# K and Q transposed in one transfer, k loaded in its own order, q on GpSimd's queue, and longer latencies in the planner, in a convolution and attention kernel on one Trainium2 core

## Chip, core and metric

The kernel runs on one core of one Trainium2 chip. A core has TensorE (PE, matrix products), VectorE (DVE), ScalarE (ACT), GpSimd (POOL) and SyncE (SP, which here only issues transfers). The engines run side by side. Each takes its own instructions in the order in which they were emitted, and waits for others by semaphores. The metric is the device time of one execution in microseconds; eleven executions of the kernel before were timed, and the median counts.

## The reference, cut to what matters

Two independent halves are computed from 2048 positions of 640 channels and written side by side. The first half is a short causal filter on k with four taps, a product with v, a long convolution over the whole sequence with a direct term, and a product with q. The second is attention with 32 heads of 20 channels in four segments of 512 positions, mixed with a running memory of the segments before.

```python
for t in range(ks):
    k_shift = k_shift + k_pad[:, t:t + S, :] * shift_k[:, ks - 1 - t][None, None, :]
kv = k_shift * v
...
y_f = kv_f * kf_f[None, :, :, :]
...
return q * (y + kv * ssm_D[None, None, :])
```

```python
for s in range(N):
    logits = jnp.einsum('bhqd,bhkd->bhqk', qs, ks) * scale + mask
    p = _softmax(logits, axis=-1)
    a_dot = jnp.einsum('bhqk,bhkd->bhqd', p, vs)
    pq = phi(qs)
    num = jnp.einsum('bhld,bhde->bhle', pq, M)
    den = jnp.einsum('bhld,bhd->bhl', pq, z)[..., None] + 1e-06
    o = g * (num / den) + (1.0 - g) * a_dot
    ...
    M = M + jnp.einsum('bhld,bhle->bhde', phi(ks), vs)
return o @ wo
```

The last lines of both excerpts are drawn together here from several lines of the reference. phi(x) is x+1 for positive x and exp(x) otherwise, and the mask admits each query only to keys at or before it.

## The kernel before

**The convolution half ("A")** goes through five groups of 128 channels. In each, `load_kv` (line 574) loads v by four transfers and k, transposed, by four. The k tile `kr` holds positions apart by their remainder modulo four, so that the filter of `kshift` (line 591) reads a contiguous run of weights. The filter is 16 products of 128 columns per block of 512 positions, against `skd`, four diagonal matrices of taps. VectorE multiplies the result with v into `vt`. `fwd` turns kv, and in the same way the filter kernel (`sk`, turned to `kT`), into a spectrum with products against the table `Wf`; ScalarE copies each result from PSUM into `F`. `bfly` adds and subtracts F into `Xh` or `Kh` on VectorE. Pointwise products and a second butterfly make `S`; `inverse` multiplies with the table `Wi`, and VectorE multiplies with q (`qd`, loaded by `load_q`, line 586, four transfers on SP) into `outa`, which GpSimd's queue stores. All large tiles exist once, `outa` twice.

**The attention half ("P" and "T")** goes through eight units: four segments times two halves of 16 heads. `proj` (line 701) makes K, Q and V of 128 positions with five products of 320 columns each. ScalarE casts them into `KQ` and `Va`. Two transfers on SP turn K into `KT` and Q into `QT`, for each of four token blocks. `bound` (line 724) works out an upper bound of the logits from the maximum of K and stores it into rows of `QT`, so that the exponential cannot overflow; `PqT` is phi of Q. `attn` (line 781) runs for four groups of four heads. It writes logits of three shapes into the PSUM tile `st`, ScalarE takes the exponential into `ET`, VectorE zeroes a triangle with `cmask`, and TensorE multiplies with V into `o`. The last shape holds key block 3 (128 columns) and key block 2 (256 columns). Its mask is added by a product of 384 columns first, of which the last 128 add zeros (line 793). VectorE divides (`rr`, `o`) and writes `o_s`; `o_s` is transposed by transfers into `oT` and multiplied with `wo`; the last segment has its own ending, `out_last` (line 851).

**The order** is not that of the loops. Every call goes to a recorder (so nearly all instructions carry one source line, 441). `price` (line 182) estimates each operation's time on its engine and its latency until another engine may use the result. `plan` (line 242) then simulates the five queues forward and backward, several times. A table `BIAS` shifts priorities of single work items and a table `HOLD` moves the time before which a load may not start; both are long lists of numbers. The best of the passes sets the order in which instructions are emitted, and which of three `ab` banks in PSUM each product gets. The plan's times are not kept at run time: only the order and the semaphores are. So an estimate that is wrong does not break anything; it lets an engine wait at an instruction while a later one would be ready.

**The queues.** SP issues nearly all loads and all transposing transfers, POOL the small constants, `Drow` and the stores of `outa` and `outb`. A wait at the head of a queue holds everything behind it.

Of the kernel before, what the change touches and what calls it, by code (L numbers as in the profile page):

```python
# [25 lines left out]
KPAD = 16  # L26
# [67 lines left out]
class Recorder:  # L94
# [87 lines left out]
    def price(self, op, method, out, ins, kw):  # L182
        n = int(np.prod(list(out.shape)[1:]))
        two = lambda a: mybir.dt.size(a.dtype) == 2
        if method == "matmul":
            if "tile_position" in kw:
                op.dur += n / 2.4 * 0.33 + (200.0 if not op.dur else 0.0)
            else:
                op.dur += max(n / 2.4 + 2.5, 27.0)
            op.lat = 260.0  # L190
# [12 lines left out]
        elif op.eng == "ACT":  # L203
            op.dur, op.lat = n / 1.152 + (33 if ins[0].space == bass.MemoryType.PSUM or n > 1000 else 95), 210.0
        elif op.eng == "DVE":
            op.stall = 115 if method == "reciprocal" else 0
            fast = all(two(a) and a.space != bass.MemoryType.PSUM and int(a.ap[-1][0]) == 1 for a in [out] + ins)
            if method == "tensor_tensor":
                op.dur = n / (1.92 if fast else 0.96) + 60
            elif method == "tensor_reduce":  # L210
                op.dur = int(np.prod(list(ins[0].shape)[1:])) / 0.96 + 60
            elif method == "reciprocal":
                op.dur = 67 + 6.1 * n
            else:
                op.dur = n / (3.84 if fast else 1.9) + 60
            op.lat = 150.0
        else:
            op.dur, op.lat = 100 + n / 1.2, 200.0
# [23 lines left out]
    def plan(self, bias, hold, passes, slack):  # L242
# [19 lines left out]
        prio = [-(o.tail + bias.get(o.key, 0)) for o in ops]  # L262
        held = [hold.get(o.key, 0) if o.dma is not None else 0 for o in ops]
        for n in range(passes + 1):
            total = self.forward(prio, held)
            if best is None or total < best[0]:
                best = (total, self.order, self.slot, self.start, self.done)
# [3 lines left out]
            lead = [end - b for b in back]  # L271
            prio = [s - (bias.get(o.key, 0) >> 3) for o, s in zip(ops, lead)]
            held = [max(0, s - slack - hold.get(o.key, 0)) if l else 0 for o, s, l in zip(ops, lead, load)]
        _, self.order, self.slot, self.start, self.done = best
        return best[0]

    @staticmethod
    def lag(o):
        return o.lat if o.dma is None else max(1150 - o.dur, -50) + o.dma + 450
# [71 lines left out]
    def forward(self, prio, held):  # L351
# [19 lines left out]
        while times:  # L371
# [3 lines left out]
            for e in free:  # L375
# [27 lines left out]
                if o.dma is not None:  # L403
                    dma_free = max(dma_free, max(t + 1150, end - 50)) + o.dma
                    fin = dma_free + 450
# [44 lines left out]
class K3:  # L450
    def __init__(self, ctx, tc, A_q, A_k, A_v, A_shift_k, A_ssm_k, A_ssm_D, B_x, B_wq, B_wk, B_wv, B_wo, B_beta, out):
# [20 lines left out]
        def const(name, arr, dt, eng=nc.gpsimd):  # L472
            t = c.tile(list(arr.shape), dt, name=name)
# [8 lines left out]
        def wload(engs, half):  # L482
            def f():
                for i, (w, eng) in enumerate(zip((B_wk, B_wq, B_wv), engs)):
                    eng.dma_start(out=self.wqkv[:, :, half, i, :], in_=w.rearrange("(cc p) j -> p cc j", p=128)[:, :, 320 * half:320 * half + 320])
# [6 lines left out]
        }  # L492
        self.skc = c.tile([128, 5, 4], bf16, name="skc")
        nc.sync.dma_start(out=self.skc[:], in_=self.shift_k.rearrange("(c p) t -> p c t", p=128))
        self.ident = const("ident", np.eye(128).astype(BF16_NP), bf16, nc.sync)
        bt = self.bt = c.tile([128, H], bf16, name="bt")
# [4 lines left out]
        self.nmask = const("nmask", np.concatenate([(cmask_np.astype(np.float32) - 1) * 30000.0] * 2 + [np.zeros((128, 128), np.float32)], axis=1).astype(BF16_NP), bf16)  # L501
        self.epsrow = const("epsrow", eps_np, f32)

        self.KQ = c.tile([128, 2, 2, 16, 32], bf16, name="KQ")
        self.PK = c.tile([128, 4, 16, 32], bf16, name="PK")
        self.Va = [c.tile([128, 4, 16, VW], bf16, name=f"Va{i}") for i in range(2)]
        self.QT = [c.tile([128, 4, L], bf16, name=f"QT{i}") for i in range(2)]
# [43 lines left out]
    def a_chunks(self, dp):  # L551
# [22 lines left out]
        def load_kv():  # L574
# [3 lines left out]
            kr = st["kr"] = self.ring("kr", [128, 4, KPAD + 512])  # L578
            nc.gpsimd.memset(kr[:, :, 0:KPAD], 0.0)
            for c in range(4):  # L580
                nc.sync.dma_start_transpose(out=kr[:, c, KPAD:KPAD + 512], in_=self.k[:, dsl].rearrange("(r c) d -> r c d", c=4)[:, c, :])
# [4 lines left out]
        def load_q():  # L586
            qd = st["qd"] = self.ring("qd", [128, 4, 4, 128])
            for b in range(4):
                nc.sync.dma_start(out=qd[:, b], in_=self.q[512 * b:512 * b + 512, dsl].rearrange("(p c) d -> p c d", c=4))

        def kshift(b):
            def f():
                kr, vt = st["kr"], st["vt"]
                ps = self.bank("ab")
                for c in range(4):
                    for t in range(4):
                        cc = (c - t) % 4
                        p0 = KPAD + 128 * b + (c - t - cc) // 4
                        nc.tensor.matmul(ps[:, 128 * c:128 * c + 128], lhsT=kr[:, cc, p0:p0 + 128], rhs=st["skd"][:, t, :], start=(t == 0), stop=(t == 3))
# [90 lines left out]
    def b_proj_chunks(self, u):  # L690
# [10 lines left out]
        def proj(tci):  # L701
            def f():
# [9 lines left out]
                if tci == 0:  # L712
                    self.KTs[u] = self.ring("KT", [128, 4, L], n=2)
                nc.sync.dma_start_transpose(out=self.KTs[u][:, :, tok], in_=KQ[:, 0, :, :])
                nc.sync.dma_start_transpose(out=QT[:, :, tok], in_=KQ[:, 1, :, :])
# [8 lines left out]
        def bound():  # L724
            kam = self.ring("kam", [128, 4], f32)
            V.tensor_reduce(out=kam[:], in_=self.KTs[u][:], axis=AX.X, op=ALU.max, apply_absolute_value=True)
            A = self.ring("A", [128, 4, 16])
            V.tensor_tensor(out=A[:], in0=self.sel[:], in1=kam[:, :, None].to_broadcast([128, 4, 16]), op=ALU.mult)
            if s > 0:
                nc.scalar.activation(out=PqT[:], in_=QT[:], func=ACTF.Exp)  # L730
                tq = self.ring("tq", [128, 4, L])
                V.tensor_scalar(out=tq[:], in0=QT[:], scalar1=1.0, scalar2=1.0, op0=ALU.add, op1=ALU.max)
                V.tensor_tensor(out=PqT[:], in0=PqT[:], in1=tq[:], op=ALU.min)
            qabs = self.ring("tq", [128, 4, L])
            V.tensor_scalar(out=qabs[:].bitcast(i16), in0=QT[:].bitcast(i16), scalar1=0x7fff, scalar2=None, op0=ALU.bitwise_and)
# [38 lines left out]
    def b_attn_chunks(self, u):  # L774
# [6 lines left out]
        def attn(g):  # L781
            def f():
# [5 lines left out]
                for spec, e0, step in ((((0, 0),), 0, -1), (((1, 0),), 512, 1), (((3, 0), (2, 128)), 896, -1)):  # L788
                    st = self.bank("st")
                    masked = e0 == 896  # L790
                    if masked:
                        for hl in range(4):
                            nc.tensor.matmul(st[:, hl, 0:384], lhsT=self.ident[:], rhs=self.nmask[:], start=True, stop=False)
                    for (kc, c0) in spec:
                        for hl in range(4):
                            rows = slice(32 * hl, 32 * hl + 32)
                            nc.tensor.matmul(st[:, hl, c0:c0 + L - 128 * kc], lhsT=KT[rows, g, 128 * kc:128 * kc + 128], rhs=QT[rows, g, 128 * kc:L],
                                             start=not masked, stop=(not masked or kc == 2), tile_position=(32 * hl, 0))
# [82 lines left out]
    ('A', 0, 0): 157004, ('A', 0, 1): 10101, ('A', 0, 10): -7597, ('A', 0, 11): 3913, ('A', 0, 12): 33761, ('A', 0, 13): -3728, ('A', 0, 14): 5624,  # L881
    ('A', 0, 15): 88348, ('A', 0, 16): 230629, ('A', 0, 17): -8128, ('A', 0, 18): -5757, ('A', 0, 19): 10830, ('A', 0, 2): 8829, ('A', 0, 20): 4481,
    ('A', 0, 21): 1304, ('A', 0, 22): -3994, ('A', 0, 23): 145, ('A', 0, 24): -576, ('A', 0, 25): -2524, ('A', 0, 26): -1099, ('A', 0, 27): -2858,
    ('A', 0, 3): 16866, ('A', 0, 4): -698, ('A', 0, 5): -458, ('A', 0, 6): 389434, ('A', 0, 7): 607, ('A', 0, 8): 3517, ('A', 0, 9): -8145,
    ('A', 1, 0): -1731, ('A', 1, 1): 3601, ('A', 1, 10): -137531, ('A', 1, 11): -176854, ('A', 1, 12): -7874, ('A', 1, 13): -16279, ('A', 1, 14): 10588,
    ('A', 1, 15): 2905, ('A', 1, 16): -7, ('A', 1, 17): -2655, ('A', 1, 18): -2590, ('A', 1, 19): -1545, ('A', 1, 2): 1649, ('A', 1, 20): 40028,
    ('A', 1, 21): 1391, ('A', 1, 22): 3816, ('A', 1, 23): -2584, ('A', 1, 24): -7, ('A', 1, 25): -2923, ('A', 1, 26): 731, ('A', 1, 27): 396,
    ('A', 1, 3): 395, ('A', 1, 4): -322, ('A', 1, 5): 12977, ('A', 1, 6): 7861, ('A', 1, 7): -1057, ('A', 1, 8): -201, ('A', 1, 9): 261,
    ('A', 2, 0): -69696, ('A', 2, 1): -2356, ('A', 2, 10): -15708, ('A', 2, 11): 257, ('A', 2, 12): -55, ('A', 2, 13): 1762, ('A', 2, 14): 6674,
    ('A', 2, 15): 491, ('A', 2, 16): 243, ('A', 2, 17): -2104, ('A', 2, 18): 175, ('A', 2, 19): 3992, ('A', 2, 2): -3416, ('A', 2, 20): 250546,  # L890
    ('A', 2, 21): -2544, ('A', 2, 22): -615, ('A', 2, 23): -563, ('A', 2, 24): -3861, ('A', 2, 25): 952, ('A', 2, 26): 5253, ('A', 2, 27): -3491,
    ('A', 2, 3): -2503, ('A', 2, 4): -4457, ('A', 2, 5): 2480, ('A', 2, 6): 5034, ('A', 2, 7): -2075, ('A', 2, 8): 243, ('A', 2, 9): -346,
    ('A', 3, 0): -36045, ('A', 3, 1): 546, ('A', 3, 10): 150040, ('A', 3, 11): -1390, ('A', 3, 12): 2538, ('A', 3, 13): -590, ('A', 3, 14): 898,
    ('A', 3, 15): 3192, ('A', 3, 16): -3627, ('A', 3, 17): -3799, ('A', 3, 18): -1242, ('A', 3, 19): 12597, ('A', 3, 2): 492, ('A', 3, 20): -88007,
    ('A', 3, 21): 959, ('A', 3, 22): -5393, ('A', 3, 23): -3393, ('A', 3, 24): -1459, ('A', 3, 25): 91621, ('A', 3, 26): 73805, ('A', 3, 27): 18751,
    ('A', 3, 3): -1299, ('A', 3, 4): -1550, ('A', 3, 5): -2302, ('A', 3, 6): 1825, ('A', 3, 7): 239, ('A', 3, 8): -4198, ('A', 3, 9): 1989,
    ('A', 4, 0): 7225, ('A', 4, 1): 3377, ('A', 4, 10): -14537, ('A', 4, 11): 1258, ('A', 4, 12): -875, ('A', 4, 13): -2828, ('A', 4, 14): -1432,
    ('A', 4, 15): 3521, ('A', 4, 16): 902, ('A', 4, 17): 30, ('A', 4, 18): -2548, ('A', 4, 19): 10489, ('A', 4, 2): -568, ('A', 4, 20): 140696,
# [107 lines left out]
```

The softmax here doesn't subtract the row's maximum and nothing guards it: scores larger than these inputs give would overflow.

## Time and profile before

| what | value |
|---|---|
| median of 11 executions | 334.29 us (329.99 to 337.91) |
| the profiled execution | 329.31 us |
| its span | 327.5 us |
| granted TensorE clock, mean | 0.986 |
| DMA traffic | 35.67 MB, mean 109 GB/s |
| packets under 512 B | 90000 of 97160 |
| KT<-KQ and QT<-KQ on SP | 32 each, 1.22 us an issue, 2.5 us to landing |
| kr<-in_A_k_dram on SP | 20, 1.26 us an issue, 2.8 us to landing |
| qd<-in_A_q_dram on SP | 20, 0.62 us an issue, 3.3 us to landing |

The span is the profiled execution from its first to its last instruction. Busy time of an engine is the time in which at least one instruction of it runs. A row of the groups gives an operation, its output and inputs, its count, its busy time, and the mean of one in ns; the means overlap their neighbours, so they sum to more than the busy time. A matmul's record includes its latency, so its rate is read from a run of them: sixteen of 128 columns take 0.90 us.

### The profile page before, as it was taken

Reading aid. Unit: us, or ns where it says so; the run is one execution under the profiler, and the core shown is the slowest. Engines: PE = TensorE matmul, PEld = TensorE weight load, DVE = VectorE, ACT = ScalarE, POOL = GpSimd, SP = SyncE. Lnnn points to the kernel's source line nnn. Section 1 sums busy time; section 2 is a strip of 40 time slices with the busy share of each in tenths; the row PEclk is TensorE's granted clock in tenths of the full one; section 3 lists DMA queues with packets and bytes.
Section 4 is the critical chain, followed back from the end, with each engine's and each line's share of the span. In section 5 each row is a group of like instructions: output and inputs, shape, how many; then the busy total and the mean of one; then the engine's idle time right before and its main releaser. Section 6 shows DMA issues by size and latency. Waiting matters only on the chain. (4 is left out here: it accounts for less than half of the span.)

```text
span 327.5 us, 8830 instructions
## 1 busy us (share of the span) xinstructions
PE 284.7 (87%) x3674; PEld 197.5 (60%) x3674; DVE 272.5 (83%) x455; ACT 265.7 (81%) x351; POOL 30.5 (9%) x58
## 2 busy tenths in 40 slices
PE   0498899989999996999999997999989988887982
PEld 0365667676777674566858664777756664654641
DVE  0016869999998979999997599999999999989842
ACT  1176799799998999899898898888899999668611
POOL 5001100000000110000101010300200002321310
PEclk9999999999999999899999999999999999998898
DMA  8945964646407987805321669513314244233262
GB/s 253 228 89 122 261 118 83 129 118 114 80 2 163 196 135 157 234 16 81 68 64 45 122 137 184 153 29 70 66 35 67 60 59 97 58 84 106 64 128 82
DMA packets 97160, 35.67 MB, mean 109 GB/s; under 512 B 90000, under 2 KB 95168, under 8 KB 96864
## 3 DMA queue, kind: packets, MB, share of 16 engines
q1 hardware_dynamic: 94816, 30.01, 44.2%
q0 software_dynamic: 1872, 4.76, 5.5%
q8 instruction: 29, 0.48, 0.6%
q10 hardware_dynamic: 432, 0.34, 0.3%
q14 instruction: 11, 0.09, 0.1%
HBM read 13.46 MB, written 5.24 MB: 57 GB/s over the span
## 5 line engine op out<-in xcount | busy, mean ns | idle before, releaser
L441 ACT ACTIVATE ET<-st 128x1536 bf16<-128x1536 f32 (+1 forms) x96 | 154.8, 1613 | 23.4 <-PE st L441 22.9
L441 PE MATMUL ab<-wqkv,xT 128*128 128x320 bf16 x480 | 76.4, 306 | 13.2 <-DMA wqkv<-in_B_wk_dram 12.4
L441 PEld LDWEIGHTS <-xT 128*128 128x128 bf16 x480 | 45.3, 100 | 33.3 <-DMA xT<-in_B_x_dram 10.4
L441 PEld LDWEIGHTS <-ET 128*128 128x128 bf16 x1280 | 42.2, 96 | 11.4 <-issue 8.1
L441 PE MATMUL o<-Va,ET 128*128 128x21 bf16 x1280 | 44.1, 173 | 3.6 <-DVE o L441 3.3
L441 ACT CAST F<-ab 128x512 bf16<-128x512 f32 x80 | 45.3, 613 | 1.8 <-PE ab L441 1.6
L441 PE MATMUL st<-QT,KT 32*128 32x128 bf16 (+3 forms) x512 | 34.9, 304 | 8.5 <-ACT ET L441 8.3
L441 ACT CAST KQ<-ab 128x320 bf16<-128x320 f32 x64 | 27.9, 459 | 15.1 <-PE ab L441 14.6
L441 DVE TENSOR_TENSOR S<-S 128x2048 bf16<-128x2048 bf16 (+1 forms) x40 | 36.9, 938 | 0.0
L441 PEld LDWEIGHTS <-Wf 128*128 128x128 bf16 x320 | 28.1, 97 | 11.2 <-issue 7.3
L441 PE MATMUL st<-nmask,ident 128*128 128x384 bf16 x128 | 26.6, 331 | 2.6 <-ACT ET L441 2.5
L441 PEld LDWEIGHTS <-KT 32*128 32x128 bf16 x512 | 11.8, 92 | 28.2 <-issue 26.3
L441 PE MATMUL ab<-kT,Wf 128*128 128x256 bf16 x160 | 23.6, 273 | 0.9 <-ACT F L441 0.2
L441 POOL DMA_DIRECT2D out_dram<-outa x20 | 15.3, 769 | 93.8 <-DVE outa L441 86.0
L441 PE MATMUL ab<-wo,oT 128*128 128x320 bf16 (+1 forms) x140 | 21.5, 292 | 2.7 <-ACT outb L441 1.7
L441 DVE TENSOR_TENSOR o<-o,rr 128x320 bf16<-128x320 f32 x48 | 23.1, 482 | 0.5
L441 DVE TENSOR_TENSOR ET<-ET,cmask 128x1024 bf16<-128x1024 bf16 x32 | 21.5, 673 | 1.8 <-ACT ET L441 1.8
L441 DVE TENSOR_TENSOR S<-Xh,Kh 128x4096 bf16<-128x4096 bf16 x10 | 22.8, 2275 | 0.0
L441 PE MATMUL ab<-vt,Wf 128*128 128x256 bf16 x160 | 22.0, 273 | 0.8 <-DVE vt L441 0.5
L441 PE MATMUL ab<-S,Wi 128*128 128x256 bf16 x160 | 20.7, 273 | 0.8 <-DVE outa L441 0.8
L441 PEld LDWEIGHTS <-oT 128*128 128x128 bf16 x160 | 13.9, 98 | 12.1 <-issue 4.9
L441 PE MATMUL ab<-skd,kr 128*128 128x128 bf16 x320 | 20.7, 219 | 0.5 <-DVE vt L441 0.4
(70 smaller groups left out, 393.5 us busy)
## 6 DMA issues: line engine op xcount, KB each, us to landing
sk<-in_A_ssm_k_dram SPq DMA_DIRECT2D x5, 512.0 KB, 4.2
vt<-in_A_v_dram SPq DMA_DIRECT2D x20, 128.0 KB, 3.1
qd<-in_A_q_dram SPq DMA_DIRECT2D x20, 128.0 KB, 3.3
out_dram<-outa POOLq DMA_DIRECT2D x20, 128.0 KB, 2.6
out_dram<-outb POOLq DMA_DIRECT2D x12, 160.0 KB, 2.9
Wf<-c_wf SPq DMA_DIRECT2D x1, 1024.0 KB
Wi<-c_wi SPq DMA_DIRECT2D x1, 1024.0 KB
wqkv<-in_B_wq_dram SPq DMA_DIRECT2D x2, 400.0 KB, 5.7
```

The costliest lines, as they stand in the source:

```text
L441: f(*[fix(a) for a in args], **{k: fix(v) for k, v in kw.items()})
```

## The change

Five edits are made at once.

1. K and Q of a token block are turned into one tile `KQT` by one transfer, where there were two. The first unit is turned by TensorE, with `ident`, into PSUM, and copied out by VectorE (K) and ScalarE (Q).
2. k is transposed by two transfers of 1024 positions in their own order. The filter reads weights with a step of four.
3. q is loaded by GpSimd's queue.
4. The mask product of the third shape has 256 columns. Key block 2's product is split into two of 128 columns, of which the second needs no mask and starts its own accumulation.
5. The planner assumes longer latencies (products 300 ns, ScalarE 320, VectorE 240 with 8 ns more for each operation, transfers 800 ns after the last packet), dearer first and cheaper later row-tiled products, applies `BIAS` and `HOLD` in one last pass after the others, and gives constants, the three weights of each half, `kr` and `skd` keys of their own. Both tables are replaced throughout.

```diff
-                op.dur += n / 2.4 * 0.33 + (200.0 if not op.dur else 0.0)
+                op.dur += n / 2.4 * 0.26 + (200.0 if not any("tile_position" in c[3] for c in op.calls[:-1]) else 0.0)
...
-            op.lat = 260.0
+            op.lat = 300.0
...
-            op.dur, op.lat = n / 1.152 + (33 if ins[0].space == bass.MemoryType.PSUM or n > 1000 else 95), 210.0
+            op.dur, op.lat = n / 1.152 + (33 if ins[0].space == bass.MemoryType.PSUM or n > 1000 else 95), 320.0
...
-            op.lat = 150.0
+            op.dur += 8
+            op.lat = 240.0
...
-        prio = [-(o.tail + bias.get(o.key, 0)) for o in ops]
-        held = [hold.get(o.key, 0) if o.dma is not None else 0 for o in ops]
+        prio = [-o.tail for o in ops]
+        held = [0] * len(ops)
...
+        return self.forward([p - bias.get(o.key, 0) for p, o in zip(prio, ops)],
+                            [max(0, t - hold.get(o.key, 0)) if l else 0 for t, o, l in zip(held, ops, load)])
...
-                    fin = dma_free + 450
+                    fin = dma_free + 800
...
-            kr = st["kr"] = self.ring("kr", [128, 4, KPAD + 512])
-            nc.gpsimd.memset(kr[:, :, 0:KPAD], 0.0)
-            for c in range(4):
-                nc.sync.dma_start_transpose(out=kr[:, c, KPAD:KPAD + 512], in_=self.k[:, dsl].rearrange("(r c) d -> r c d", c=4)[:, c, :])
+            kr = st["kr"] = self.ring("kr", [128, KPAD + S])
+            nc.gpsimd.memset(kr[:, 0:KPAD], 0.0)
+            for n in range(2):
+                nc.sync.dma_start_transpose(out=kr[:, KPAD + 1024 * n:KPAD + 1024 * n + 1024], in_=self.k[1024 * n:1024 * n + 1024, dsl])
...
-                nc.sync.dma_start(out=qd[:, b], in_=self.q[512 * b:512 * b + 512, dsl].rearrange("(p c) d -> p c d", c=4))
+                nc.gpsimd.dma_start(out=qd[:, b], in_=self.q[512 * b:512 * b + 512, dsl].rearrange("(p c) d -> p c d", c=4))
...
-                        nc.tensor.matmul(ps[:, 128 * c:128 * c + 128], lhsT=kr[:, cc, p0:p0 + 128], rhs=st["skd"][:, t, :], start=(t == 0), stop=(t == 3))
+                        first = KPAD + 512 * b + c - t
+                        nc.tensor.matmul(ps[:, 128 * c:128 * c + 128], lhsT=kr[:, first:first + 509:4], rhs=st["skd"][:, t, :], start=(t == 0), stop=(t == 3))
...
-                nc.sync.dma_start_transpose(out=self.KTs[u][:, :, tok], in_=KQ[:, 0, :, :])
-                nc.sync.dma_start_transpose(out=QT[:, :, tok], in_=KQ[:, 1, :, :])
+                self.KTs[u] = self.KQT[half][:, 0]
+                if u > 0:
+                    nc.sync.dma_start_transpose(out=self.KQT[half][:, :, :, tok].rearrange("p i g t -> p (i g) t"), in_=KQ.rearrange("p i h d -> p (i h d)"))
+                else:
+                    for i in range(2):
+                        ps = self.bank("ab")
+                        for g in range(4):
+                            nc.tensor.matmul(ps[:, 128 * g:128 * g + 128], lhsT=KQ[:, i, 4 * g:4 * g + 4, :], rhs=self.ident[:], start=True, stop=True)
+                        (V.tensor_copy if i == 0 else nc.scalar.copy)(out=self.KQT[half][:, i, :, tok], in_=ps[:].rearrange("p (g t) -> p g t", g=4))
...
-                            nc.tensor.matmul(st[:, hl, 0:384], lhsT=self.ident[:], rhs=self.nmask[:], start=True, stop=False)
-                    for (kc, c0) in spec:
+                            nc.tensor.matmul(st[:, hl, 0:256], lhsT=self.ident[:], rhs=self.nmask[:], start=True, stop=False)
+                    parts = [(kc, c0, 0, L - 128 * kc) for kc, c0 in spec] if not masked else [(3, 0, 0, 128), (2, 128, 0, 128), (2, 128, 128, 256)]
```

What this makes of the order, as it stands in the lists of instructions of the two kernels: SP begins with Wf, sk, xT, wq, wk, ident, wv before, and with wk, wq, xT, wv, ident, skc, sk after, Wf following as the ninth. ScalarE's last copy of F for the first butterfly of kv has 45 of its instructions ahead before, and 76 after. VectorE's first butterfly of the filter kernel has 8 ahead before, and 41 after. In the end of the list, two of the last four `outa` products stand behind the last `o_s` after the change, where all four stood ahead.

## The prediction

> **What bounds the kernel now.** I read the page's busy times first, then busy time by stretch, then the waits, then the chain that ended last, and the start and the end of the timeline.
>
> ```profile
> PE 284.7 (87%) x3674; PEld 197.5 (60%) x3674; DVE 272.5 (83%) x455; ACT 265.7 (81%) x351; POOL 30.5 (9%) x58
> ...
> 12.44:46.50 34.06, 30.37 (x307) 21.69 (x306) 17.26 (x34) 24.84 (x45) 2.28 (x5) 1.00 0.66 147
> 46.50:315.70 269.20, 249.56 (x3338) 173.47 (x3335) 253.28 (x417) 238.01 (x302) 23.67 (x38) 0.99 0.47 97
> 315.70:327.50 11.80, 4.73 (x35) 2.24 (x33) 1.96 (x4) 1.60 (x4) 0.21 (x1) 0.90 0.38 96
> ```
>
> Three engines are above 80%, so the whole span says little. The stretches do: each line has the stretch, its length, then PE, PEld, DVE, ACT and POOL busy. Before 46.5 us VectorE worked 17.26 us; from there, the first butterfly of kv, to the last write of o_s at 315.7 it worked 253.28 of 269.20 us, 94.1%, against PE's 92.7% and ACT's 88.4%. So in the long stretch VectorE is nearest to its limit, PE just behind.
>
> ```profile
> PE ab L441 <- DMA wqkv<-in_B_wk_dram: 12.4, 1, 12.4
> DVE rr L441 <- PE o L441: 6.6, 10, 2.2
> DVE outa L441 <- PE ab L441: 3.3, 5, 1.2
> ACT PqT L441 <- DMA QT<-KQ: 2.8, 3, 1.1
> DVE kam L441 <- DMA KT<-KQ: 0.8, 1, 0.8
> ```
>
> The waits, from the whole trace (total, times, longest): one start of 12.4 us for weights, and about 10 us in which VectorE waits for PE's attention and inverse products. Waits for the transposed K and Q are small: 2.8 and 0.8 us.
>
> ```profile
> PE 19%; DVE 11%; ACT 4%; DMA 3%; issue 2%; DVEq 0%; SPq 0%; ACTq 0%
> ...
> 1.63 5.67 SPq L441 DMA_TRANSPOSE xT<-in_B_x_dram  x1
> 7.36 0.57 SPq L441 DMA_DIRECT2D wqkv<-in_B_wq_dram  x1
> 7.98 0.52 SPq L441 DMA_DIRECT2D wqkv<-in_B_wk_dram  x1
> ...
> 46.51 1.23 DVE L441 TENSOR_TENSOR Xh<-F 128x2048 bf16<-128x2048 bf16 x1 [0.64 <-ACT F L441]
> ```
>
> The chain, which reaches back only to 200 us, has 3% of the span in DMA and none in SP's queue: unloading SP is worth little by itself. The timeline shows the start: xT's issue holds SP for 5.67 us and the first weights come behind it. Its last line is the butterfly, released by ScalarE's last copy of F.
>
> **The Trainium skill.** Three places bear on this.
> - "TensorE: Matmul & The Clock Gate", Part 3 (The mechanism): products on different row groups of the array run together. The trace agrees: four 32-row products of 512 columns take 0.28 to 0.33 us from their start to the next work.
> - "SBUF — State Buffer", the trap on DVE and DMAs of the GpSimd queue: GpSimd writes those descriptors and is locked out while VectorE runs in a 2-port mode. The trace shows a little at most: out_dram<-outa takes POOL 750 ns at least and 944 at most.
> - "DMA: Bandwidth & Descriptors", Issuing engines are not separate DMA queues: another queue saves only sequencer time, because all share the same DMA engines. For qd that time is 20 issues, 14.0 us summed on SP's timeline. The sharing itself no view of mine isolates.
>
> **The change part by part.**
>
> *Mask columns.* Four mask products of 384 columns take 0.81 us with a record of 0.33, so they follow at (0.81-0.33)/3 = 0.16 us; 256 columns at the same rate take 0.107. 128 of them save 128 x 0.053 = 6.8 us of PE. Against it, key block 2's product is split: 12 instructions replace 8, with the same columns. The 8 took 0.28 us from start to next work, so three fours take 0.28 to 0.42; over 32 groups that is 0 to 4.5 us, and I take 1.5. PE: -5.3 us.
>
> *First unit on TensorE.* 32 products of 128 columns at 0.056 (16 of kr's take 0.90): +1.8 us PE. Four VectorE copies of PSUM at 0.69 (row of ET<-st, 128x512), after overlap with neighbours 2.5 us; four ScalarE copies at 0.61, 2.2 us. All lie before 30 us, where VectorE is mostly idle. They save the first unit's eight transfers of 1.2 us on SP.
>
> *One transfer for K and Q.* 56 issues of 1.22 us become 28 of twice the size. This size is not in the trace; it lies between 1.22 (no dearer) and 2.44 (no saving). xT is five times KT's size and takes 2.75 to 3.25, so interpolation gives about 1.6. Q lands later by 0.4, never earlier than K's old transfer plus its own. Since the waits for both sum to 3.6 us, I book 0, bounds -2 to +2.
>
> *k in its own order.* Twenty issues of 1.25 become ten of about 1.6. TensorE now reads weights at a step of four elements. sk is read so already: 113 ns a load against 98 for kr, but four take 0.26 us and sixteen of kr 0.90, both near 0.05 apart. Cost 0, bound 320 x 0.015 = 4.8 us.
>
> SP's timeline, summed, is 209 us; these parts and qd take about 67 off. It is hidden already, so 0.
>
> *qd on POOL.* Twenty issues of 0.76 add 15 us to POOL's 30.5. In the new order each group of four after the first stands between outa stores of the channel group before. They wait for that group's last multiplication, since qd has one buffer, and up to 3 us of stores queue behind. outa has two buffers, and the next inverse comes tens of us later. Cost 0; if a late qd held the inverse, VectorE would wait behind it, up to 2 us for each of five groups.
>
> *Start.* SP's new order is wk, wq, xT, wv, and only then sk and Wf (1.5 MB, ahead of xT before). xT issues at about 1.9 us instead of 1.63 but with less in front. It landed 8.7 us after its issue; without Wf and sk I take 6.3, bounds 4.5 and 8.7. The first product comes at 8.2 us instead of 12.44, and the first cast at 9.7.
>
> *Order.* This decides. I count work ahead of marks in each engine's instruction list, mean durations scaled so that totals meet busy times (ACT 0.885, DVE 0.902). Before's first butterfly of kv has 16.7 us of VectorE work ahead by this count; 17.26 were measured. In the changed list it has 28.3, because k's butterfly, two bounds and more attention stand ahead. Its last F copy stands behind 46.6 us of ScalarE work counted from the first cast (before: 24.8).
>
> ScalarE's 16.4 us ahead of the first exponential are paced by PE: 75 projection products at 0.139, 32 turns, 16 of sk, 20 of kT, bound and memory, 17.1 us, at 85% 20, so the first exponential is at 28.5. The remaining 30.2 at 97% (it ran at 99% from 34.7 to 46.5) end at 59.6; I take 59.0. VectorE has then idled 59.0-28.3 = 30.7 us, against 46.5-17.3 = 29.2: a 1.5 us loss.
>
> From there to o_s VectorE has 272.5+2.5-28.3-3.2 = 243.5 us; the 3.2 are the last copies and two outa products that now stand after o_s, under the transfer of oT. At 94.1% that takes 258.8 us. But more attention and projection is done by then: PE has 281.2 less 46 (8.2 to 59 at 91%) less 5 for the tail = 230 us left, 0.945 of VectorE's work instead of 0.985, and ScalarE 218, 0.90 instead of 0.94. If PE can be filled to 92.7% as before, VectorE reaches 243.5/(230/0.927) = 98.1%. Dependences will not let all of it come; I take halfway, 96.1%, or 253.4 us.
>
> *Sum.* 59.0+253.4 = 312.4, plus the unchanged tail of 11.8 = 324.2 us of span, 326.0 with the 1.8 around it, against 329.3: -3.3. The profiled execution was below all eleven timed runs. I carry the difference to their median: 334.3-3.3 = **331.0 us**.
>
> **Rivals.**
> - *Late butterfly, slower.* If ScalarE holds F back behind the exponentials of the first unit, the first butterfly comes at 62.5, and if VectorE's share stays 94.1% the sum is 62.5+258.8+11.8+1.8 = 334.9, +5.6, median 339.9. For it: the changed list has about 30 ScalarE instructions more ahead of that F. Against it: PE and ScalarE have less left. It decides from 57 us on at the old share, or below 94.9% at 59.
> - *No change.* Longer assumed latencies only shuffle the list, VectorE's share becomes 94.9%, and 59.0+256.6 puts o_s back at 315.6: 334.3.
> - *Full release.* xT early, first butterfly at 56.5, VectorE at 98.1%: 56.5+248.2+13.6 = 318.3, -11.0, median 323.3. Stretches at 97 to 99% between 60 and 100 and 200 and 260 us of the old trace speak for it; single buffers for S, F, vt and qd against.
>
> **How the numbers follow.** Forecast 0.46 (its own range 328 to 333.5), full release 0.12, no change 0.13, late butterfly 0.29. Under 0.5%, 1.7 us, this kernel's measurement tells nothing from no change. The forecast's range crosses that a little, so faster 0.55, same 0.15, slower 0.30. The range 321.5 to 339.5 reaches from full release to the late butterfly and takes in qd's and the weight loads' bounds.
>
> **What would show it.** PE busy near 281, DVE 275; first product near 8 us; first Xh<-F near 59; VectorE's share from there to the last o_s near 96%; waits for KQT under 5 us; POOL issues of qd under 1 us. A share under 95%, a first butterfly after 61, or inverses that wait for qd make the forecast wrong.

## The result and the profile after

The changed kernel took 335.34 us (median of 12 executions, 333.58 to 338.15), beside 333.05 us for the kernel before (47 executions). The ratio is 1.0094, 95% interval 1.0064 to 1.0124: slower by about 1%, where 331.0 us and a gain were forecast. Ratios, here and below, are taken over the executions within 1.5% of each kernel's fastest, which leaves out more of the kernel before than of the others, so they can lie up to 0.9% above the ratio of the medians. The profiled execution took 335.37 us, its span is 333.6 us.

The page of the changed kernel, busy times and the granted TensorE clock in 40 slices:

```profile
PE 284.8 (85%) x3834; PEld 202.0 (61%) x3834; DVE 275.9 (83%) x459; ACT 268.3 (80%) x355; POOL 46.3 (14%) x78
...
PEclk9999999999799999999699999999999999997598
```

VectorE and ScalarE do what was forecast (275 and about 268), and POOL's 16 us more are qd. TensorE was to fall to 281 and stayed at 284.8. The clock row has a dip in its eleventh slice, one in its twentieth and a longer one near the end.

Busy time by stretch, cut at the marks of the prediction: first product, first exponential, first butterfly of kv, end of the last o_s. The columns are those explained in the prediction, and the one after POOL is the granted clock.

```profile
0.00:11.07 11.07, 0.00 (x0) 0.00 (x1) 0.00 (x0) 1.28 (x1) 5.38 (x17) 1.00 0.81 187
11.07:33.18 22.11, 21.61 (x168) 14.56 (x169) 10.30 (x23) 15.55 (x35) 0.00 (x0) 1.00 0.47 154
33.18:64.02 30.84, 29.52 (x419) 21.29 (x418) 18.82 (x36) 29.99 (x42) 1.09 (x3) 1.00 0.77 138
...
64.02:321.20 257.18, 228.13 (x3204) 162.66 (x3203) 243.44 (x394) 219.87 (x275) 38.36 (x56) 0.95 0.47 92
321.20:333.60 12.40, 5.50 (x47) 3.47 (x45) 3.38 (x7) 1.61 (x4) 1.50 (x2) 0.89 0.34 95
```

The first butterfly comes at 64.0 us, not 59.0. From there VectorE has 243.44 us of work, as counted (243.5), and does it in 257.2 us, a share of 94.7% where 96.1% was taken; the kernel before had 94.1%. The tail is 12.4 us instead of 11.8. So the 9.4 us between the forecast span (324.2) and the measured one are 5.0 of a late butterfly, 3.8 of share, and 0.6 of tail. A first butterfly after 61 us and a share under 95% were both on the prediction's list of signs that it is wrong.

Between the medians the miss is only 4.3 us (335.34 for 331.0). The profiled execution of the kernel before lay 5.0 us under the median of its eleven, and that of the changed kernel lies at its own, so the two profiles differ by more than the two kernels do.

TensorE had 228.13 us of work in the long stretch, where 230 were counted, and was busy for 88.7% of it; the kernel before had 92.7%. So VectorE was not held up by more work on TensorE than was forecast. Both engines waited more.

The waits over the whole trace (total, times, longest), those that answer to the prediction's:

```profile
PE ab L442 <- DMA xT<-in_B_x_dram: 11.1, 1, 11.1
...
DVE rr L442 <- PE o L442: 6.8, 10, 2.1
...
DVE outa L442 <- DMA out_dram<-outa: 2.3, 1, 2.3
...
ACT KQ L442 <- DMA KQT<-KQ: 1.8, 1, 1.8
...
DVE tq L442 <- DMA KQT<-KQ: 0.9, 1, 0.9
...
ACT PqT L442 <- DMA KQT<-KQ: 0.5, 1, 0.5
```

The start now waits for xT instead of weights. The waits for KQT sum to 3.2 us, about what those for K's and Q's separate transfers did before (3.6). One new wait, 2.3 us of VectorE for the store of outa, lies in the tail. The chain of work that ended last tells more of KQT than the waits do:

```profile
DVE 35%; PE 31%; ACT 15%; DMA 11%; issue 6%; SPq 1%; POOL 0%; DVEq 0%; ACTq 0%; POOLq 0%
PE ab L442 22%; DVE S L442 9%; ACT ET L442 7%; DMA KQT<-KQ 6%; PE st L442 5%; DVE Xh L442 5%; PE o L442 4%; DMA xT<-in_B_x_dram 3%; ACT F L442 3%; DVE Kh L442 3%; DVE ET L442 2%; DVE o L442 2%; DVE F L442 2%; DVE outa L442 2%; DVE kam L442 2%
```

For 6% of the span, some 20 us, it runs through the transfer KQT<-KQ. Small waits do not put a transfer off the path. (This chain reaches back to the start; that of the kernel before reached only to 200 us, so the shares of the two cannot be compared.)

### The profile page after: what moved, and what is told of

Its sections match the earlier page's. It is cut to its first block, busy times and chain, and to the rows that moved or that the text cites. A ratio compares the mean times of both kernels' runs of the same rounds, so it can differ in the third digit from the quotient of the medians.

```text
span 333.6 us, 9034 instructions
## 1 busy us (share of the span) xinstructions
PE 284.8 (85%) x3834; PEld 202.0 (61%) x3834; DVE 275.9 (83%) x459; ACT 268.3 (80%) x355; POOL 46.3 (14%) x78
## 4 chain that ended last, share of the span: by engine, by line
DVE 35%; PE 31%; ACT 15%; DMA 11%; issue 6%; SPq 1%; POOL 0%; DVEq 0%; ACTq 0%; POOLq 0%
PE ab L442 22%; DVE S L442 9%; ACT ET L442 7%; DMA KQT<-KQ 6%; PE st L442 5%; DVE Xh L442 5%; PE o L442 4%; DMA xT<-in_B_x_dram 3%; ACT F L442 3%; DVE Kh L442 3%; DVE ET L442 2%; DVE o L442 2%; DVE F L442 2%; DVE outa L442 2%; DVE kam L442 2%
## 5 line engine op out<-in xcount | busy, mean ns | idle before, releaser
L442 ACT CAST F<-ab 128x512 bf16<-128x512 f32 x80 | 44.0, 604 | 3.0 <-PE ab L442 2.9
L442 ACT CAST KQ<-ab 128x320 bf16<-128x320 f32 x64 | 26.7, 437 | 20.5 <-PE ab L442 18.2
L442 PE MATMUL st<-KQT 32*128 32x128 bf16 (+2 forms) x640 | 36.1, 283 | 6.7 <-ACT ET L442 6.5
L442 PEld LDWEIGHTS <-KQT 32*128 32x128 bf16 x640 | 13.2, 93 | 24.2 <-issue 22.1
L442 PE MATMUL st<-nmask,ident 128*128 128x256 bf16 x128 | 20.0, 280 | 8.6 <-ACT ET L442 8.6
L442 PE MATMUL ab<-vt,Wf 128*128 128x256 bf16 x160 | 22.7, 278 | 1.1 <-DVE xm L442 0.9
L442 PE MATMUL ab<-S,Wi 128*128 128x256 bf16 x160 | 21.5, 280 | 0.0
L442 DVE RECIPROCAL rr<-o 128x16 f32<-128x16 f32 (+1 forms) x64 | 15.2, 238 | 6.8 <-PE o L442 6.8
L442 PEld LDWEIGHTS <-kr 128*128 128x128 bf16 x320 | 19.1, 114 | 2.4 <-issue 2.1
```

Source lines behind the costliest of these rows:

```text
L442: f(*[fix(a) for a in args], **{k: fix(v) for k, v in kw.items()})
```

## The experiments

All ratios are to the kernel before, executed on the same chip in turn with each experiment. Experiments 1 to 4 ran on one chip, 5 to 8, 9 and 10, 11 and 12, and 13 to 16 on others. Ratios from different chips are less certain than their intervals say: e11 and e16 are the same kernel, with medians of 331.70 and 332.23 us, and their ratios are 0.993 (0.990 to 0.997) and 1.000 (0.998 to 1.003). Where an order is kept while the code is edited, the planner's call is replaced by a list:

```diff
-    rec.plan(BIAS, HOLD, PASSES, SLACK)
+    rec.fixed(ORDER)
```

**Order and edits apart.** e1 has all edits (with the first unit turned by transfer too) in the old order. e2 and e3 are the same code, with one kernel's order up to the first Xh and the other's for the rest.

> All five code edits (one KQ transfer, k in its own order, q on GpSimd's queue, the narrower mask, and the first unit also by transfer instead of TensorE), but every operation stands where the kernel before has it in its order. Theory 1 (the order of the ramp costs, the edits are neutral or a small gain): 0.98 to 1.00 of the time before, first Xh near 46.5 us, VectorE's share after it near 94%. Theory 2 (the edits cost: longer landing of KQT, q on GpSimd, weights at a step): 1.005 to 1.015, with waits for KQT above 6 us. Theory 3 (a lower granted clock, brought by the edits): the clock is 0.96 here too and PE's busy time does not fall below 284 us.

> The same code as e1. The order is that of the kernel before up to the four butterflies that write the first Xh, and that of the changed kernel for all that is left. Theory 1 (the ramp of the new order costs): first Xh near 46.5 us, at or below e1's time, 0.98 to 0.995 of before. Rival (the long stretch of the new order costs): 1.00 to 1.02, more than e1, VectorE's share after the first Xh under 94%. Theory 2: as in e1, about 1.01.

> The same code as e1. The order is that of the changed kernel up to the four butterflies that write the first Xh, and that of the kernel before for what is left. Theory 1: first Xh near 64 us, 1.005 to 1.02 of before, more than e1 and e2. Rival (the long stretch of the new order costs): 0.98 to 1.00. Theory 2: about 1.01, like e1.

Measured: e1 1.037 (1.031 to 1.043), e2 1.038 (1.033 to 1.043), e3 1.074 (1.069 to 1.080). The edits in the old order cost four times what the whole change costs. Theory 2 had the waits for KQT, but not this size. The waits of VectorE in e1:

```profile
DVE kam L456 <- DMA KQT<-KQ: 9.5, 4, 4.3
DVE kam L456 <- issue: 7.9, 3, 4.1
```

kam, the maximum of K, stands in the old order where K's own transfer landed early. Now K comes with Q, and VectorE waits 17.4 us in all at this instruction (before: 1.4), with all its later work behind. For 9.5 us of that the profile names KQT's transfer, for 7.9 it shows no releaser. The signs of theory 3 are there as well: the clock is 0.958 over all executions, and TensorE's busy time 284.2 us. But e5 below, without the single transfer, has 0.987 and 279.6 us, so the low clock came with the waits and not with the other edits.

e2 and e3 carry the same wait (5.6 and 19.1 us) and a seam between two orders, so they don't decide between ramp and long stretch. One thing e2 does show: its first Xh came at 46.9 us, but the first S<-Xh,Kh, the product made of it, only at 82.1 (70.7 in the changed kernel), and it took 346.8 us. An early first butterfly gains nothing where the work behind it does not move up.

**The start.** e4 is the changed kernel with this edit and SP's order as the expectation says:

```diff
-            nc.sync.dma_start_transpose(out=xT[:], in_=self.x[L * s:L * s + L, :])
+            for t in range(4) if s == 0 else ():
+                nc.sync.dma_start_transpose(out=xT[:, :, 128 * t:128 * t + 128], in_=self.x[128 * t:128 * t + 128, :])
```

> The changed kernel with the first segment's xT brought by four transfers of 128 positions instead of one of 512, in SP's order xT0, wk, xT1, wq, wv, xT2, xT3. All else as changed. If the 5 us that the first butterfly came too late stem from the landing of xT, the first product comes at 6.5 to 8 us instead of 11.1, the first Xh 3 to 4 us earlier than 64.0, and the time is 0.997 to 1.002 of before (after: 1.009). If the ramp is held by ScalarE and dependences instead, the first product comes earlier but the first Xh by under 1 us, and the time stays within 1.005 to 1.012.

Measured: 0.997 (0.994 to 1.000), 332.72 us. SP's first issues (start, length), of the changed kernel and then of e4:

```profile
0.74 0.46 SPq L442 DMA_DIRECT2D wqkv<-in_B_wk_dram  x1
1.25 0.51 SPq L442 DMA_DIRECT2D wqkv<-in_B_wq_dram  x1
1.82 5.70 SPq L442 DMA_TRANSPOSE xT<-in_B_x_dram  x1
```

```profile
0.74 1.32 SPq L456 DMA_TRANSPOSE xT<-in_B_x_dram  x1
2.11 0.57 SPq L456 DMA_DIRECT2D wqkv<-in_B_wk_dram  x1
2.74 1.21 SPq L456 DMA_TRANSPOSE xT<-in_B_x_dram  x1
```

The one large transfer is issued at 1.82 us and released the first product at 11.07, 9.2 us later. With a quarter of it, TensorE starts at 6.97 us, released by wk. The first Xh comes at 61.3 us instead of 64.0; of 4.1 us at the start 2.7 arrive there, a little less than the 3 to 4 expected, in part because TensorE then waits 0.8 us for wq. The gain is 1.2% by the ratios and 0.8% by the medians (332.72 for 335.34 us, other chips), and fits the first reading. e4 changes two things at once, though: its transfers are smaller, and the first of them stands ahead of all weights. One whole xT in first place was not run, so which of the two counts is not shown.

**Which edit needs which order.** e5 is e1 without the single KQ transfer. e6 is the changed kernel with two transfers again. e7 has q on SP, e8 is the kernel before with the mask edit alone.

```diff
-                    nc.sync.dma_start_transpose(out=self.KQT[half][:, :, :, tok].rearrange("p i g t -> p (i g) t"), in_=KQ.rearrange("p i h d -> p (i h d)"))
+                    for i in range(2):
+                        nc.sync.dma_start_transpose(out=self.KQT[half][:, i, :, tok], in_=KQ[:, i, :, :])
```

> The kernel before, in its own order, with the narrower mask, k in its own order and q on GpSimd's queue, but with K and Q in two transfers as before. In e1 the maximum of K (kam) waited 17.4 us for KQT where it waited 1.4 us before. If the single transfer is what made e1 slow, the time is 0.985 to 1.00 and kam waits under 2 us. If q on GpSimd or k's weights at a step did it, 1.02 to 1.04 as e1.

> The changed kernel in its order, with K and Q of all units but the first in two transfers into KQT, K's right behind its cast and Q's where the single one stands. If the single transfer still costs in the new order, 0.995 to 1.005 of before (after: 1.009). If the new order has already hidden its landing (waits for KQT sum to about 3.5 us in the trace of after), 1.005 to 1.013.

> The changed kernel in its order with q loaded on SP, at the same places of the list. If qd on GpSimd's queue costs (late stores of outa and late qd), 0.998 to 1.006. If it was free, as predicted, 1.007 to 1.014.

> The kernel before in its own order with the narrower mask alone. The prediction's 5.3 us less of TensorE work, in an order that waits for VectorE in the long stretch: 0.99 to 1.00 of before, PE busy 279 to 281 us. If the work that is saved comes back through a lower granted clock, PE busy stays near 284 us and the time at 0.997 to 1.003.

Measured: e5 0.993 (0.990 to 0.997), kam waits 1.2 us. e6 1.033 (1.026 to 1.039), outside both expectations. e7 1.012 (1.006 to 1.018). e8 0.998 (0.995 to 1.002), TensorE busy 278.9 us.

In the old order the single transfer is more than the whole loss: e1 against e5 is 4.4% by the ratios, and e5, with the other three edits, is faster than the kernel before. What of it is the later landing, what the wait for Q's cast, and what the tile that K and Q now share, no run separates. In the new order the single transfer is worth about 2%: e6 took 341.78 us, and e7, which equals the changed kernel in time, 335.34 on the same chip. SP's timeline shows where most of this arises. In the ramp of e6 the eight half-size issues where four stood keep SP busy nearly without a gap, and what stands behind them slips. The same issue, the bound's rows for the second unit, in the changed kernel and in e6:

```profile
52.60 0.62 SPq L442 DMA_DIRECT2D KQT<-bT  x1
```

```profile
36.48 4.41 SPq L456 DMA_TRANSPOSE KQT<-KQ  x3
...
47.57 4.72 SPq L456 DMA_TRANSPOSE xT<-in_B_x_dram  x1
52.38 3.01 SPq L456 DMA_TRANSPOSE kr<-in_A_k_dram  x2
...
56.93 0.62 SPq L456 DMA_DIRECT2D KQT<-bT  x1
```

It comes 4.3 us later, TensorE's weight loads wait 2.6 us for kr, and the first Xh is at 68.2 us, 4.2 later than in the changed kernel. I placed K's transfer right behind its cast; another place might cost less, so the 2% is what the single transfer is worth against this placement.

q on GpSimd is free within the interval. The mask edit takes 5.8 us off TensorE and nothing off the kernel that the ratio shows; the medians (331.57 for 333.90 us) leave room for 0.7%. k in its own order and q on GpSimd's queue together did gain in the old order: on the same chip, with 22 executions each, e5 took 329.49 us and e8, which lacks them, 331.57. Resampling the executions puts this at 0.2 to 1.0%.

**The start in the old order.** e9 is e5 with xT in four and the weights ahead of Wf and sk, edited as e4.

> e5 (old order, narrower mask, k in its own order, q on GpSimd's queue, K and Q in two transfers) with the first segment's xT in four transfers and SP starting with xT0, wk, xT1, wq, wv, xT2, xT3, ident, sk, Wf. If the start is on the path as e4 showed in the new order, the first product comes near 7 us instead of 12.4 and the time is 0.975 to 0.985 of before (e5: 0.993). If the old order's ramp is held by sk and Wf, which now come later, the first Xh stays near 46.5 us and the time at 0.99 to 1.00.

Measured: 0.993 (0.990 to 0.996), as e5. The first product comes at 6.4 us, but TensorE then waits 2.5 us for wq and 3.0 for sk, and the first Xh is at 48.6 us instead of e5's 47.4. The second reading holds: the old order feeds its ramp with what was pushed back.

**The granted clock.** Over all executions its mean was 0.959 for the changed kernel, 0.979 to 0.980 for the kernel before, 0.987 for e5. Two stretches of the changed kernel, and what lies around them:

```profile
80.00:84.00 4.00, 0.96 (x19) 0.32 (x16) 3.97 (x4) 3.45 (x3) 2.67 (x4) 1.00 0.78 188
84.00:89.00 5.00, 4.63 (x46) 2.90 (x47) 4.21 (x11) 2.37 (x4) 0.00 (x0) 0.66 0.04 13
89.00:160.00 71.00, 62.77 (x915) 45.27 (x912) 68.78 (x111) 66.43 (x84) 7.16 (x11) 1.00 0.56 109
160.00:168.00 8.00, 7.36 (x74) 3.84 (x74) 7.78 (x15) 6.05 (x8) 0.77 (x1) 0.57 0.01 2
```

TensorE is busy for 0.96 of the 4 us from 80 to 84, because it waits for an exponential of ScalarE and then for the bound (A); near 156 us it waits for an exponential once, for longer:

```profile
82.11 0.40 PE L442 MATMUL st<-KQT 32*128 32x512 bf16 x4 [1.55 <-ACT ET L442]
84.36 1.10 PE L442 MATMUL ab<-tq,A 128*16 128x512 bf16 x4 [1.85 <-DVE A L442]
...
158.28 0.60 PE L442 MATMUL st<-nmask,ident 128*128 128x256 bf16 x4 [2.79 <-ACT ET L442]
```

Then the clock is at half for some 3.4 us (a mean of 0.66 over 5), and VectorE, fully busy until then, idles for 0.8 of 5 us. The Trainium skill, "TensorE: Matmul & The Clock Gate", Part 1 (The HAM clock gate), says that an idle window of about 3.4 us halves the clock, and a busy one restores it. The trace agrees in length, and shows that TensorE need not be idle for that long: two gaps of 1.55 and 1.85 us with 0.4 us of work between them sufficed, and one of 2.79. In the kernel before the clock falls at 130 us, after one gap of 2.27.

What decides is a fixed grid of windows. In every profiled execution, each stretch at half or at full clock, from the first entry of the clock in the trace to the last fall, lasts a whole multiple of 3.413 us. Cut into such windows from that entry on, all eighteen executions together show this: after a window at full clock in which TensorE was busy for less than 46% the clock was halved (36 of 36), after one of more than 72% never (0 of 1392), and between the two it went both ways (19 of 109). At half clock, a window under 89% busy left it halved (53 of 53). Where the grid lies differs between executions, so the same gap may or may not matter: the changed kernel has no fall after a gap of 1.74 us at 274 us, and e13, with the same instructions, has one after 1.75 us at 278.

The longest fall lies near the end of the changed kernel, and no run removed it:

```profile
300.00:317.00 17.00, 9.68 (x137) 5.91 (x136) 16.89 (x26) 11.27 (x9) 2.40 (x4) 0.61 0.19 53
```

From 303.6 to 317.3 us the clock is at half, and as long or longer in e4 and in each of e10 to e16; the kernel before has 3.4 us there. VectorE is busy for 16.89 of the 17 us, so what this fall costs can't be read from the stretch, and it was not tested.

e10 is e4 with products that nothing reads added near 80 and 156 us; e12 is e10 with wq earlier. e11 and e14 to e16 put them into the changed kernel itself, and e13 is their base, without them.

```diff
+    rec.add_banks("warm", [rec.slots["o"][0]])
+    for i, n in enumerate(WARM):
+        rec.key = ("warm", i)
+        ps = rec.bank("warm")
+        for _ in range(n):
+            rec.nc.tensor.matmul(ps[:, 384:512], lhsT=K.ident[:], rhs=K.ident[:], start=True, stop=True)
```

WARM is (34, 18, 42): 34 and 18 products ahead of the first two instructions shown above, 42 ahead of the third (e14 has only the first two numbers, e15 only the last). They write columns of the bank `o` that are otherwise unused.

> e4 (changed kernel with xT in four) with 94 products of ident with ident added, whose result nothing reads, at the places where TensorE waited 1.3 to 2.8 us just before its granted clock fell to 0.5: 52 of them near 78 to 82 us, 42 near 153 us. If the halved clock costs time, it stays at 1.00 from 80 to 90 and from 155 to 165 us and the time is 0.990 to 0.996 of before (e4: 0.997). If VectorE is the bound where the clock falls, the clock stays up as well but the time stays at 0.995 to 1.001.

> The changed kernel itself (xT in one transfer) with the same 94 unread products at the same two places of its list as in e10, and nothing else. If the fall of the granted clock at 84 and 160 us is part of what VectorE's share lost, the mean clock rises from 0.96 to about 0.97 and the time is 1.002 to 1.006 of before (after: 1.009). If the clock falls only where VectorE is the bound, 1.007 to 1.012.

> e10 with wq issued ahead of the second quarter of xT (SP: xT0, wk, wq, xT1, wv, xT2, xT3). In e4 TensorE waited 0.81 us for wq after its first five products. If that wait is on the path, the first Xh comes 0.5 to 0.8 us earlier than 60.6 and the time is 0.989 to 0.994 of before. If the second quarter of xT is late instead, 0.994 to 1.000.

> The changed kernel with its own order written out instead of planned: the same instructions. It is the base for e14 to e16 on the same chip: 1.005 to 1.013 of before, clock 0.953 to 0.963.

> e13 with the 52 unread products near 80 us only. The fall of the clock at 84 us left VectorE idle for 0.8 us of the four after it. If that fall costs time, 1 to 2.5 us less than e13. If VectorE's later idle time swallows it, less than 0.7 us.

> e13 with the 42 unread products near 156 us only. VectorE was 0.97 to 1.00 busy while the clock was down there, so 0 to 0.7 us less than e13 if VectorE is what bounds that stretch; 1.5 us or more if TensorE's backlog is met later, in the stretch of 220 to 240 us, where VectorE idles 4.6 us.

> e13 with all 94 products, as e11. By the medians of e10 and e11 3.5 us less than e13, that is 0.998 to 1.001 of before. If the ratios' smaller figure holds, 0.5 to 1 us less.

| run | us | ratio | 95% interval | mean clock |
|---|---|---|---|---|
| e10 | 329.35 | 0.995 | 0.992 to 0.998 | 0.975 |
| e11 | 331.70 | 0.993 | 0.990 to 0.997 | 0.972 |
| e12 | 329.33 | 0.984 | 0.978 to 0.989 | 0.974 |
| e13 | 336.00 | 1.013 | 1.008 to 1.017 | 0.957 |
| e14 | 332.90 | 1.002 | 1.000 to 1.005 | 0.965 |
| e15 | 334.03 | 1.007 | 1.005 to 1.010 | 0.966 |
| e16 | 332.23 | 1.000 | 0.998 to 1.003 | 0.970 |

By the ratios e10 gained 0.2% over e4 and e11 1.6% over the changed kernel, on different chips (by the medians 3.4 and 3.6 us); e13 to e16 settle it on one. Against e13, products at the first place save 3.1 us, at the second 2.0, at both 3.8, though the 94 add 5.3 us of TensorE work (94 at 0.056). e11, e12 and e14 gained more than was expected of them. No run put such products where the clock did not fall. The same stretches in e16:

```profile
80.00:84.00 4.00, 3.52 (x57) 2.98 (x55) 3.97 (x5) 3.50 (x3) 2.16 (x3) 1.00 0.87 192
84.00:89.00 5.00, 4.96 (x69) 3.28 (x68) 4.97 (x11) 3.90 (x7) 0.00 (x0) 1.00 0.03 7
...
160.00:168.00 8.00, 6.66 (x76) 3.56 (x73) 7.90 (x17) 6.14 (x9) 0.86 (x1) 0.79 0.01 2
```

The clock stays up from 84 to 89 us (and for part of the second stretch), and VectorE is busy 4.97 of 5 us instead of 4.21. At the second place VectorE was the bound at once (7.78 of 8 us); what is saved there must show later, and where is open. The expectation for e15 had 0 to 0.7 us or 1.5 and more; 2.0 speaks for TensorE's backlog being met later, but on top of the first place the second adds only 0.7 us (e16 against e14).

In e12 the first Xh came at 61.6 us, not below 60.6: TensorE now waited 0.9 us for wv, and its slow start (see below) lasted to 15.4 us where it ended at 12.5 in e10. It takes what e10 takes; the lower ratio goes with a slower chip, where the kernel before had 335.06 us. By its ratio it is faster than the kernel before, by 1.6%, and its median is 6.0 us below the changed kernel's. But e5 and e9, in the old order and with two transfers, have nearly the same medians, 329.49 and 329.96 us: with its start and two of its clock falls mended, the new order does what the old one does with three of the five edits. From the first Xh to the last o_s of e12:

```profile
61.60:315.60 254.00, 230.50 (x3297) 166.82 (x3296) 243.50 (x394) 220.01 (x275) 38.00 (x56) 0.97 0.48 94
```

VectorE's share is 243.50/254.00 = 95.9%, nearly the 96.1% of the prediction, from a butterfly 2.6 us later than forecast.

## Why the prediction was wrong, step by step

*Mask.* Right: -5.8 us of TensorE (e8) for -5.3, and hidden as far as the ratio shows. The split costs next to nothing: the record of its 12 products is 0.35 us, that of the 8 before was 0.34.

*First unit on TensorE.* Its own costs were not isolated. TensorE's work between first product and first exponential was 21.6 us, though, where 17.1 were summed. The term most mis-sized is the 75 projection products at 0.139 = 10.4 us. They sum to 13.5, because only the third fifteen run at their later pace throughout:

```profile
11.07 4.18 PE L442 MATMUL ab<-wqkv,xT 128*128 128x320 bf16 x15 [11.07 <-DMA xT<-in_B_x_dram]
...
15.90 2.71 PE L442 MATMUL ab<-wqkv,xT 128*128 128x320 bf16 x15
...
19.18 2.20 PE L442 MATMUL ab<-wqkv,xT 128*128 128x320 bf16 x15
```

The trace of the kernel before showed this too: its first ten take 2.83 us. This slow start is very likely the halved clock again. The trace has no entry of the clock before 16.93 us, where the views, for want of one, show 1.00 (so their means leave it out); the first entry, at full clock, begins there, and the pace changes in just those fifteen products. In e4 both come at 14.2 us, in the kernel before at 18.0. A second error hid the first. TensorE was busy for 98% of this stretch, where 85% was taken, so that 22.1 us came near the 20.3 forecast. That was luck.

*One transfer for K and Q.* The issue is cheaper than taken (1.25 us, no more than half the size took), the landing later (3.6 us for 2.5, not 0.4 more). Booked at 0 with bounds of 2 us, it is worth some 6 us in the new order (e6 against e7) and costs 15 to 18 us in the old one (e1 against e5, by ratios and by medians). The step read the waits of the kernel before as the price of lateness. Those waits are small because that order was made for those landings; they say nothing of another order, nor of another landing in the same one.

*SP, hidden already, so 0.* False of the ramp of the new order, as e6 shows, and perhaps of the old one too, where e5 gained 2.1 us over e8 with fewer issues on SP. The sum behind it does not hold either: a row of SP's timeline that joins several issues includes the gaps between them (six of oT in one row of 18.91 us), so 209 us is too much, and the parts as priced, 33 for K and Q, 9 for k and 14 for qd, make 56 and not 67.

*k in its own order, qd.* A k load's record is 114 ns for 98. Moving q back to SP changes nothing in the new order (e7), so qd's 0 stands there. In the old order the two edits together gained 2.1 us (e5 against e8), so their 0 was a little too low; how it divides between them is open. e7 fits the sentence of "DMA: Bandwidth & Descriptors" that the prediction names, that another queue saves only sequencer time. Of the trap on GpSimd's queue nothing was seen (753 ns an issue, 903 at most).

*Start.* This is the first step that failed. Of the landing of xT, 6.3 us was taken with bounds 4.5 and 8.7, from the thought that less stood in front. It took 9.2. Less in front removed nothing: 800 KB of weights stood ahead of it where 1.5 MB of Wf and sk had, and a later segment's xT in the same trace, with no weights ahead, still took 6.6 us or more. Smaller transfers, the first ahead of the weights, did bring the first product to 7 us (e4). The first product is late by 2.9 us, the stretch to the first exponential is 22.1 us for 20.3, and both together are nearly all of the 5.0 us. About 1 us of this is the chance of one execution. In the seven profiles with this same start (the changed kernel, e7, e11, e13 to e16) the clock's first entry comes between 14.25 and 16.93 us and the first Xh, in the same sequence, between 62.95 and 64.02; the changed kernel's profile is the last of the seven.

*Order.* ScalarE's 30.5 us from the first exponential to the butterfly were 30.8, so the count of work ahead was right. The result looks like the rival "late butterfly", but not its mechanism: ScalarE held F no longer than the forecast said. The share is the second step that failed. "Halfway" between 94.1 and 98.1% supposed that TensorE could be filled nearly as before, to about 91% (230 us in 253.4), at the clock of before. It was filled to 88.7%. The new order leaves TensorE waiting for ScalarE and the bound near 82 and 156 us, and the clock falls. Keeping it busy there gave 3.8 us back (e16), the size of the miss in the share. That the two are the same 3.8 us is not shown: in e16's profiled execution the long stretch is only 1.0 us shorter than in the changed kernel's, 256.2 us at a share of 95.1%. What took the rest of the share stays open; the third fall of the clock is one candidate.

*Tail.* +0.6 us; the wait for a store of outa lies there, which was not in the list of late things.

## What to carry to other kernels

Price a cheaper or later transfer against the order that will run, not against the waits of the order that was fitted to the old one: the same edit was worth -2% and +4% here. When an order is changed, look for gaps of TensorE of about 2 us, and for shorter ones close together, even if another engine is the bound there: here the clock was halved after windows of 3.4 us in which TensorE was busy for under about half, and filling them at two places saved time. For a first load that everything waits for, try smaller transfers, the first of them in front; less ahead of the whole one did not help here.

## What was not expected of the hardware

One transposing transfer of 512 positions held SP's queue for 5.70 us at the start, and landed 9.2 us after its issue with 800 KB of weights ahead of it, as against 8.7 us with 1.5 MB ahead in the kernel before. The same transfer for later segments takes 2.9 to 4.0 us of issue in the changed kernel. In quarters the first two issues are 1.32 and 1.21 us. A transfer from SBUF to SBUF of 128x1024 elements takes SP as long (1.25 us) as one of 128x512 (1.22).

Filling the gaps at two places with 94 products whose results nobody reads took 3.8 us, 1.1%, off the changed kernel (e13 to e16). The clock of TensorE went by windows of 3.413 us, and a window in which it was busy for under 46% always cost at least one more at half clock. The first fifteen products take nearly twice the time of later ones though the views show a clock of 1.00 there: the trace's first entry of the clock comes only after them, and the pace changes with it.
